# A third buffer for the filter's values, sines four steps behind their phases, and the second step's loads issued with the first step's

## The chip, the cores and the metric

The kernel runs on one core of a Trainium2 chip. The time is the device time of one execution in microseconds (us). The kernel before has a median of 3793.43 us over 7 executions (3792.16 to 3796.14). A profile records one execution: which instruction ran when on each engine, and what ended each wait. The engines are TensorE (PE: matrix products; PEld is its weight load), VectorE (DVE), ScalarE (ACT), GpSimd (POOL), and SyncE (SP), which does nothing here but start the DMA transfers. SP takes its instructions strictly in turn: a transfer whose wait is not over holds all that stand behind it (SPq in the profile's rows).

## The reference

```python
B, S, D = 4, 12480, 128
h_filt = (np.maximum(pos_emb @ w1, 0.0) @ w2) * np.exp(-0.01 * pos)[:, None]
u = x * v
Uf = np.fft.rfft(u, n=2 * S, axis=1)
Hf = np.fft.rfft(h_filt, n=2 * S, axis=0)
y = np.fft.irfft(Uf * Hf[None], n=2 * S, axis=1)[:, :S, :]
z = (x * y).reshape(B * S, D)        # 49920 rows of 128
h = z @ moe_w_in                     # 128 -> 2048
g = h * np.cos(h)
out = g @ moe_w_out                  # 2048 -> 128
```

A long convolution of `u` with a filter along the sequence, for each of 128 channels and 4 batches, and then a two-layer network with `h * cos(h)` between its layers.

## The kernel before

**The convolution by matrix products.** The Fourier transform over the sequence is done in two steps, each a set of matmuls with tables of sines and cosines: N1 = 96 by N2 = 120 points. Forward: the first step (`f1_units`, matmul at line 402) goes over 64 groups of two channels, called b here, and evicts each result from PSUM into the large tile `slots` (lines 415 to 422; for the filter into `ftile` and `slots`, lines 424 to 435). The second step (`f2_units`) goes over 48 pairs of frequencies k1: a matmul with a matrix `w` that also holds the twiddle factors (line 442), and the complex product with the filter's values `h` (lines 458 and 460 on DVE, the sum at 461 on POOL). Backward: `i1_units` (line 466) and `i2_units` (line 491) in the same manner; the latter's result is multiplied by `x` and written to the DRAM tensor `zd`.

**Stages in order.** 0 to about 62 us: layers that make the filter in time, in part beside `u = x * v` of batch 0 (lines 390 and 396). About 64 to 118 us: first step of the filter; the evictions go to ACT for a share of 0.53 of the b's and to DVE for the others. Beside it the last u tiles are made, and then the tables for the backward transform (`inverse_tables`): POOL makes the phases of ten sines (lines 200 to 217), and ACT does a sine of each (line 226). The class `Tables` keeps a list of phases that wait for their sine; when the list has `lag` entries, the oldest is put onto ACT's stream. One step of `inverse_tables` is taken for every fifth yield of the first step, so where a sine stands among ACT's evictions is set when the program is written out. About 122 to 168 us: first step of batch 0. About 168 to 274 us: `f2_both_units`, the second step of batch 0 and of the filter at once. There ACT and DVE make `w` (lines 289 and 291), PE multiplies both (lines 442, 445, 448), ACT evicts the filter's values to an SBUF tile `h` (line 614), DVE and POOL form the product, and SP writes `w` to `wd` (line 603) and `h` to `hd` (line 616) in DRAM, from where the later batches load them. `w` and `h` have two buffers each. About 274 to 340 us: `i1_units` of batch 0.

**The network and the other batches.** From about 340 us on, the network runs over 98 row tiles of 16 chunks each, one step per chunk: `moe_up` (matmul 725, ACT 728, DVE 731, POOL 734), one step later `moe_act` (ACT 739, DVE 741), and `LAG` = 4 steps later `moe_down` (matmul 750). With every step, the loop takes as many units of the convolution of the later batches as a running account (`owed`) allows; each unit says how many steps it is worth. So the order of every engine's stream is written out by hand, by generators, and no scheduler changes it. In that part the convolution uses three PSUM banks, `cv`. The entry into `f2_units` comes three times, near 756, 1579 and 2400 us.

**What f2_units does at its start.** `units` first runs `before(j)` for the first `ahead` = 2 indices, which issues loads of `w` and `h` on SP (lines 581 and 583), then yields, and in its loop issues those of index j + 2 while it does index j. Its pool has three buffers of each.

**How an output tile leaves.** `moe_evict` copies the accumulated tile to `ot`; `moe_store`, called at chunk 8 of the next row tile, transposes it (matmuls at line 126), copies it to `ob` on ACT (line 765) and issues the stores to `out` on SP (line 773). `ob` has one buffer. The load of the rows of `zd` for a later tile (line 709, `zb`) is issued at chunk 12.

Of the kernel before, what the change touches and what calls it, by code (L numbers as in the profile page):

```python
# [9 lines left out]
F32 = mybir.dt.float32  # L10
# [6 lines left out]
P = 128  # L17
# [13 lines left out]
def kernel(  # L31
# [46 lines left out]
    nc = tc.nc  # L78

    B, S, D = x.shape  # L80
    FO = pos_emb.shape[1]
    DFF = moe_w_in.shape[1]
    N1, N2 = 96, 120
# [15 lines left out]
    NFC = DFF // P  # L99
# [151 lines left out]

    def inverse_tables(pool):

        t = Tables(pool, nc.gpsimd, 2)
        part = t.whole([P, 1], [[1, 1]], channel_multiplier=1, name="part")
        part4 = t.whole([P, 1], [[1, 1]], base=1, channel_multiplier=4, name="part4")
        step = t.whole([P, P], [[1, P]], name="step")
        mid = t.whole([P, P], [[1, P]], base=-MID, name="mid")
        cs, rows, tw_t = back_tables(pool)
        yield from t.sines(step, part, N2, [(cs[:, 0, 0:H + 1], 1), (cs[:, 1, 0:H + 1], 0)],  # L260
                           eighths=slice(0, H + 1, H))
        yield from t.sines(step[:, 1:H], part, N2,
                           [(cs[:, 0, H + 1:], 0), (cs[:, 1, H + 1:], 1)])
        yield from t.sines(step, part4, 4 * N1,
                           [(rows[:, i, :], q) for i, q in enumerate((0, 1, 2, 3))])
        yield from t.sines(mid, part4, TURN, [(tw_t[:, 0, :], 1), (tw_t[:, 1, :], 0)],
                           eighths=slice(H - 1, N2, H))
        t.finish(1)
        for kept, made in ((csd, cs), (rowsd, rows), (twd, tw_t)):
            nc.sync.dma_start(kept[:, :, :], made[:, :, :])  # L270

    def back_tables(pool):

        cs = pool.tile([N2, 2, N2], F32, name="cs")
        rows = pool.tile([N1, 4, R], F32, name="rows")

        tw_t = pool.tile([N1, 2, N2], F32, name="tw_t")
        return cs, rows, tw_t
# [18 lines left out]
    def make_w(w, k1, **how):  # L297


        turn(w, even[:, 0, :], even[:, 1, :], tw_w[:, 0, k1:k1 + 1], tw_w[:, 1, k1:k1 + 1],  # L300
             **how)
# [98 lines left out]
    def f1_mm(ps, u, b, i):  # L400

        nc.tensor.matmul(ps[0:KE, i * 2 * N1:(i + 1) * 2 * N1], u[:, b, 0:KE, i],  # L402
                         c1[0:u.shape[0], :, :].rearrange("p r k -> p (r k)"),
                         start=True, stop=True)
# [161 lines left out]
    def f1_units(bank, u, share=0.5, evict=f1_evict):  # L566
        def mm(j, ps, i):
            if i == 0:
                ps = bank()
            f1_mm(ps, u, j, i)  # L570
            return ps

        return units(CB, F1_STEPS, lambda j: None, mm, lambda j, ps: evict(ps, j, share), 2)

    def f2_units(bank):
        with tc.tile_pool(name="there", bufs=3) as pool:
            ws, hs = {}, {}

            def before(j):
                ws[j] = pool.tile([KE, 2, N2], F32, name="w")  # L580
                nc.sync.dma_start(ws[j][:, :, :], wd[j, :, :, :])
                hs[j] = pool.tile([N2, 2, 2, D], F32, name="h")
                nc.sync.dma_start(hs[j][:, :, :, :], hd[j, :, :, :, :])

            def mm(j, ps, i):
                if i == 0:
                    ps = bank()
                f2_mm(ps, ws[j], 2 * j, i)
                return ps

            yield from units(N1 // 2, F2_STEPS, before, mm,
                             lambda j, ps: f2_product(pool, ps, hs.pop(j), 2 * j), 4)

    def f2_both_units(bank):

        with tc.tile_pool(name="both", bufs=2) as pool:
            ws = {}

            def before(j):
                ws[j] = pool.tile([KE, 2, N2], F32, name="w")  # L600
                for i in range(2):
                    make_w(ws[j][:, i, :], 2 * j + i, half=bank)
                nc.sync.dma_start(wd[j, :, :, :], ws[j][:, :, :])

            def mm(j, ps, i):
                if i == 0:
                    ps = bank(), bank()
                for filt in range(2):
                    f2_mm(ps[filt], ws[j], 2 * j, i, filt=filt == 1)
                return ps  # L610

            def after(j, ps):
                h = pool.tile([N2, 2, 2, D], F32, name="h")
                nc.scalar.activation(h[:, :, :, :].rearrange("p g r d -> p (g r d)"),
                                     ps[1][0:N2, :], AF.Copy, scale=1.0 / M)
                nc.sync.dma_start(hd[j, :, :, :, :], h[:, :, :, :])
                yield from f2_product(pool, ps[0], h, 2 * j)

            yield from units(N1 // 2, F2_STEPS, before, mm, after, 4, ahead=1)
# [69 lines left out]

    def forward_units(bank, back):  # L690

        yield from f1_units(bank, slots[0:R, :, :, :])
        yield from f2_units(bank)
        next(back)
        yield from i1_units(bank)

# [3 lines left out]
    def first_row(n):  # L700
        return min(R + (n - 1) * P, NROWS) if n else 0
# [54 lines left out]
        nc.scalar.copy(out=ot[:, 0:m], in_=accs.pop(n)[:, 0:m])  # L756
        return ot

    def moe_store(pool, n, ot):
        m = rows_of(n)  # L760
        pt = ps_h.tile([P, BANK], F32, name="ph")
        for i in range(G):
            transpose(pt[0:m, i * D:(i + 1) * D], ot[:, i * m:(i + 1) * m], ident)
        ob = pool.tile([P, 2, UA * D], F32, name="ob", bufs=1)
        nc.scalar.copy(out=ob[0:m, :, :].rearrange("p h n -> p (h n)"), in_=pt[0:m, :])
        row = first_row(n)
        while row < first_row(n + 1):
            b, g, n1 = row // R // NG, row // R % NG, row % R
            count = min(R - n1, first_row(n + 1) - row)
            first, _, second, _ = n2s(g)  # L770
            start = out[b * S + n1 * N2 + first, :]
            at = row - first_row(n)
            nc.sync.dma_start(
                bass.AP(tensor=start.tensor, offset=start.offset,
                        ap=[[N2 * D, count], [(second - first) * D, 2], [1, UA * D]]),
                ob[at:at + count, :, :])
            row += count

    with tc.manual_schedule():
        with tc.tile_pool(name="psum", bufs=8, space=PSUM) as psum, \  # L780
                ExitStack() as first:
            def bank():
                return psum.tile([P, BANK], F32, name="ps")
# [5 lines left out]
            aT = above.rearrange("p b j i -> p b (j i)")  # L789


            keep = first.enter_context(tc.tile_pool(name="keep", bufs=1, side="right"))
            w2_sb = keep.tile([P, 2 * D], F32, name="w2_sb")
            nc.gpsimd.memset(w2_sb[:, :], 0.0)
            with tc.tile_pool(name="layers", bufs=1, side="right") as pool:
                w1_sb = pool.tile([P, P], F32, name="w1_sb")
# [42 lines left out]
            for _ in first_u:  # L839
                for _ in range(2):  # L840
                    next(f1)
            with tc.tile_pool(name="tables", bufs=1) as pool:
                sines = inverse_tables(pool)
                for i, _ in enumerate(f1):
                    if i % 5 == 0:
                        next(sines, None)
                for _ in sines:
                    pass
# [39 lines left out]
        mpool = ctx.enter_context(tc.tile_pool(name="moe", bufs=2))  # L888
# [20 lines left out]
            next(conv)  # L909
        moe_turn(mpool, 0)  # L910
        steps = [(n, c) for n in range(NALL) for c in range(NFC)]
        hidden, gates, ots = {}, {}, {}
        for i in range(len(steps) + LAG):
            if i < len(steps):
                n, c = steps[i]
                if n == 0 and c == NFC // 2:
                    load(1)
                if c == NFC - 4 and n + 2 < NALL:
                    load(n + 2)
                hidden[i] = moe_up(mpool, n, c)  # L920
            if 0 <= i - 1 < len(steps):
                gates[i - 1] = moe_act(mpool, *hidden.pop(i - 1))
            if i >= LAG:
                pn, pc = steps[i - LAG]
                moe_down(pn, pc, gates.pop(i - LAG))
                if pc == NFC - 1:
                    ots[pn] = moe_evict(mpool, pn)
            if i < len(steps):

                if c == (LAG - 1 if n else NFC - 2) and n + 1 < NALL:  # L930
                    moe_turn(mpool, n + 1)
                if c == NFC // 2 and n - 1 in ots:
                    moe_store(mpool, n - 1, ots.pop(n - 1))
            owed += 1.0
            while owed > 0.0:
                owed -= next(conv, owed)
        for n in sorted(ots):
            moe_store(mpool, n, ots[n])
# [1 line left out]
_INS = ['x', 'v', 'pos_emb', 'w1', 'w2', 'moe_w_in', 'moe_w_out']  # L940
_OUTS = [((49920, 128), 'float32')]
# [25 lines left out]
```

## Time and profile before

| | us |
|---|---|
| median of 7 executions | 3793.43 (3792.16 to 3796.14) |
| the profiled execution's own time | 3792.16 |
| its span, first to last instruction | 3790.3 |
| mean granted clock of TensorE | 0.993 of full |
| h's evictions (line 614), 48 | 28.7 busy, 598 ns each |
| writes to hd and wd, 48 each | 240.0 KB and 116.2 KB each |
| matmuls of line 442 in the later batches | 173.6 busy, 381 ns each |
| SP's waits for ob before the stores, 56 | 1308.2 in all |

A row of the profile names the line, the engine, the operation, the tile written and those read, and how many; in brackets stands how long the engine was idle before it and what released it. In a list of waits a row reads: engine, tile and line that waited, what it waited for, and then the total us, how many times and the longest. A `DMA hd<-h` as releaser means that the transfer's arrival ended the wait. The granted clock (PEclk) is the share of full speed that the chip allowed TensorE. A line such as L126 or L226 is that of a helper that several callers use. Most matmuls appear as two records. Idle time of an engine counts only where nothing else sets the end of that stretch.

### The profile page before, as it was taken

To read this page: it belongs to the slowest core of one execution; us is meant where nothing else is said; L and a number is where in the kernel's file an instruction comes from. 1 tells how busy PE (TensorE), PEld (TensorE's weight loads), DVE (VectorE), ACT (ScalarE), POOL (GpSimd) and SP (SyncE) were. 2 spreads that over 40 slices of the span, in tenths; PEclk is the share of its full clock that TensorE was granted. 3 is DMA by queue.
4 is the path that set the end of the run, shared out by engine and by line. 5 is a ranking of instruction groups with operands and counts; after the bars stand their busy time and mean duration, and the time that the engine had idled before them with its cause. 6 is when DMAs were issued, how large, how long until landed. Compare 5 with 4: busy or idle time off the path is not lost.

```text
span 3790.3 us, 47246 instructions
## 1 busy us (share of the span) xinstructions
PE 3703.5 (98%) x13546; PEld 2109.3 (56%) x13546; DVE 2771.2 (73%) x5658; ACT 2519.7 (66%) x4683; POOL 2592.0 (68%) x2342
## 2 busy tenths in 40 slices
PE   7898999999999999999999999999999999999999
PEld 6777555645466555555565556555566544444444
DVE  8887887678876887778766787788765566666666
ACT  5756776766665557766655567666664677777777
POOL 6666886478854665688845664788644577777776
PEclk9999999999999999999999999999999999999999
DMA  6253541022201550122203540222105300000000
GB/s 166 73 175 100 150 149 52 12 80 75 76 23 54 176 174 20 36 79 78 61 12 104 180 122 12 62 78 78 42 12 163 91 18 22 17 18 22 17 21 15
DMA packets 209499, 276.14 MB, mean 73 GB/s; under 512 B 17111, under 2 KB 146535, under 8 KB 209111
## 3 DMA queue, kind: packets, MB, share of 16 engines
q1 hardware_dynamic: 209239, 273.12, 24.4%
q8 instruction: 109, 1.79, 0.2%
q14 instruction: 151, 1.24, 0.1%
HBM read 193.64 MB, written 79.42 MB: 72 GB/s over the span
## 4 chain that ended last, share of the span: by engine, by line
PE 82%; POOL 7%; DVE 4%; ACT 3%; DMA 2%; issue 2%; SPq 0%; POOLq 0%; ACTq 0%; DVEq 0%
PE ph L725 31%; PE acc L750 26%; PE cv L750 5%; PE cv L491 5%; PE cv L466 4%; POOL f L734 4%; PE cv L402 3%; PE cv L442 3%; PE ph L126 2%; PE ps L402 2%; DMA hd<-h 1%; DVE k L731 1%; ACT cs L739 1%; POOL tm L295 1%; PE ps L466 1%
## 5 line engine op out<-in xcount | busy, mean ns | idle before, releaser
L734 POOL TENSOR_TENSOR f<-a,k 128x512 f32<-128x512 f32 (+1 forms) x1568 | 1988.7, 1268 | 1057.1 <-DVE k L731 1054.4
L725 PE MATMUL ph<-at,w_in_sb 128*128 128x512 f32 (+1 forms) x3136 | 1601.7, 592 | 5.2 <-DVE gt L741 4.6
L728 ACT ACTIVATE a<-ph,quarter 128x512 f32<-128x512 f32 (+1 forms) x1568 | 1073.3, 685 | 761.3 <-PE ph L725 752.0
L750 PE MATMUL acc<-gt,w_out_sb 128*128 128x512 f32 (+1 forms) x2688 | 1373.8, 593 | 10.1 <-ACT ot L756 9.8
L741 DVE TENSOR_TENSOR gt<-ph,cs 128x512 f32<-128x512 f32 (+1 forms) x1568 | 1077.2, 687 | 318.9 <-ACT cs L739 292.4
L731 DVE TENSOR_SCALAR k<-a 128x512 f32<-128x512 f32 (+1 forms) x1568 | 769.5, 491 | 628.4 <-ACT a L728 607.6
L739 ACT ACTIVATE cs<-f 128x512 f32<-128x512 f32 (+1 forms) x1568 | 980.3, 625 | 333.4 <-POOL f L734 330.8
L750 PEld LDWEIGHTS acc<-gt,w_out_sb 128*128 128x128 f32 x2688 | 505.9, 189 | 663.4 <-issue 619.8
L725 PEld LDWEIGHTS ph<-at,w_in_sb 128*128 128x128 f32 x3136 | 554.4, 190 | 338.5 <-issue 269.7
L461 POOL TENSOR_TENSOR slots<-slots,t 120x256 f32<-120x256 f32 x384 | 311.7, 818 | 62.7 <-DVE t L460 27.0
L491 PEld LDWEIGHTS cv<-slots,tm 96*104 96x104 f32 x1920 | 240.9, 170 | 107.3 <-issue 84.1
L491 PE MATMUL cv<-slots,tm 96*104 96x128 f32 x1920 | 254.4, 275 | 8.5 <-DVE tm L291 4.9
L750 PE MATMUL cv<-gt,w_out_sb 128*128 128x512 f32 (+1 forms) x448 | 224.5, 583 | 0.7 <-DVE gt L741 0.7
L466 PEld LDWEIGHTS cv<-cs,slots 120*96 120x96 f32 x1536 | 176.7, 167 | 67.6 <-issue 65.7
L466 PE MATMUL cv<-cs,slots 120*96 120x120 f32 x1536 | 183.1, 266 | 0.0
L442 PE MATMUL cv<-slots,w 124*120 124x256 f32 x576 | 173.6, 381 | 6.6 <-DMA w<-wd 6.6
L442 PEld LDWEIGHTS cv<-slots,w 124*120 124x120 f32 x576 | 103.8, 184 | 130.6 <-issue 117.7
L402 PEld LDWEIGHTS cv<-c,slots 104*124 104x124 f32 x768 | 132.5, 192 | 71.2 <-issue 58.3
L402 PE MATMUL cv<-c,slots 104*124 104x192 f32 x768 | 151.2, 326 | 4.8 <-DVE gt L741 3.5
L750 PEld LDWEIGHTS cv<-gt,w_out_sb 128*128 128x128 f32 x448 | 84.9, 190 | 104.5 <-issue 99.5
L390 DVE TENSOR_TENSOR xt<-xt,vt 104x256 f32<-104x256 f32 x177 | 137.2, 782 | 0.2 <-DMA vt<-in_v_dram 0.2
L476 DVE TENSOR_TENSOR slots<-cv,other 96x240 f32<-96x240 f32 x384 | 133.7, 394 | 4.2 <-ACT other L474 4.2
(129 smaller groups left out, 2581.8 us busy)
## 6 DMA issues: line engine op xcount, KB each, us to landing
h<-hd SPq DMA_DIRECT2D x144, 240.0 KB
tm<-td SPq DMA_DIRECT2D x96, 312.0 KB
xt<-in_x_dram SPq DMA_DIRECT2D x120, 208.0 KB
vt<-in_v_dram SPq DMA_DIRECT2D x120, 208.0 KB
xs<-in_x_dram SPq DMA_DIRECT2D x120, 208.0 KB
zd<-zs SPq DMA_DIRECT2D x119, 208.0 KB
zb<-zd SPq DMA_DIRECT2D x96, 256.0 KB
w<-wd SPq DMA_DIRECT2D x144, 116.2 KB
```

Source lines behind the costliest of these rows:

```text
L402: nc.tensor.matmul(ps[0:KE, i * 2 * N1:(i + 1) * 2 * N1], u[:, b, 0:KE, i], c1[0:u.shape[0], :, :].rearrange("p r k -> p (r k)"), start=Tr ...
L442: nc.tensor.matmul(pi, w[:, i, :], parts[0:KE, :, k], start=True, stop=True)
L461: nc.gpsimd.tensor_tensor(y[:, r], y[:, r], t[:, r], op=op)
L466: nc.tensor.matmul(ps[0:N1, (i * 2 + r) * N2:(i * 2 + r + 1) * N2], parts[0:N2, r, :, b, i], cs[:, r, :], start=True, stop=True)
L491: nc.tensor.matmul(ps[0:R, i * D:(i + 1) * D], t[:, i, r, :], slots[0:N1, :, place, :], start=(r == 0), stop=(r == 1))
L725: nc.tensor.matmul(ph[:, 0:m], w_in_sb[:, c * P:(c + 1) * P], ats[n][:, 0:m], start=True, stop=True)
L728: nc.scalar.activation(a[:, 0:m], ph[:, 0:m], AF.Identity, bias=quarter[:, 0:1], scale=INV_TWO_PI)
L731: nc.vector.tensor_scalar(out=k[:, 0:m], in0=a[:, 0:m], scalar1=ROUND, scalar2=ROUND, op0=ALU.add, op1=ALU.subtract)
L734: nc.gpsimd.tensor_tensor(f[:, 0:m], a[:, 0:m], k[:, 0:m], op=ALU.subtract)
L739: nc.scalar.activation(cs[:, 0:m], f[:, 0:m], AF.Sin, scale=TWO_PI)
L741: nc.vector.tensor_tensor(gt[:, 0:m], ph[:, 0:m], cs[:, 0:m], op=ALU.mult)
L750: nc.tensor.matmul(accs[n][:, 0:m], w_out_sb[:, c, :], gt[:, 0:m], start=(c == 0), stop=(c == NFC - 1))
```

## The change

Four edits. In `f2_both_units`, `h` has three buffers instead of two; `w` keeps two. In `inverse_tables`, the list of waiting phases holds four entries instead of two, so each sine stands two entries later in ACT's stream, and at the end all that are left are put there together. The tile `w2_sb`, which the filter's layers use, moves to a pool on the other side of SBUF and is given back ahead of the tables, whose `turned` tile has five buffers instead of three. In `forward_units`, the generator of the second step is started ahead of the first step, so the first two pairs of loads of `w` and `h` are issued on SP before the first step's matmuls. And `moe_store` is split: transposes and the copy to `ob` stay at chunk 8 (`moe_back`), and the stores on SP are issued at chunk 10. The order of instructions on PE, DVE and POOL is the same in both kernels; on ACT only the ten sines stand elsewhere, and on SP only these loads and stores.

```diff
     def inverse_tables(pool):
-        t = Tables(pool, nc.gpsimd, 2)
+        t = Tables(pool, nc.gpsimd, 4)
...
-        t.finish(1)
+        t.finish(len(t.waiting))
...
             def after(j, ps):
-                h = pool.tile([N2, 2, 2, D], F32, name="h")
+                h = pool.tile([N2, 2, 2, D], F32, name="h", bufs=3)
...
     def forward_units(bank, back):
+        f2 = f2_units(bank)
+        next(f2)
         yield from f1_units(bank, slots[0:R, :, :, :])
-        yield from f2_units(bank)
+        yield from f2
         next(back)
         yield from i1_units(bank)
...
-    def moe_store(pool, n, ot):
+    def moe_back(pool, n, ot):
         m = rows_of(n)
         pt = ps_h.tile([P, BANK], F32, name="ph")
         for i in range(G):
             transpose(pt[0:m, i * D:(i + 1) * D], ot[:, i * m:(i + 1) * m], ident)
         ob = pool.tile([P, 2, UA * D], F32, name="ob", bufs=1)
         nc.scalar.copy(out=ob[0:m, :, :].rearrange("p h n -> p (h n)"), in_=pt[0:m, :])
+        return ob
+
+    def moe_store(n, ob):
         row = first_row(n)
...
-            keep = first.enter_context(tc.tile_pool(name="keep", bufs=1, side="right"))
-            w2_sb = keep.tile([P, 2 * D], F32, name="w2_sb")
+            keep = tc.tile_pool(name="keep", bufs=1)
+            w2_sb = keep.__enter__().tile([P, 2 * D], F32, name="w2_sb")
...
             for _ in first_u:
                 for _ in range(2):
                     next(f1)
+            keep.__exit__(None, None, None)
             with tc.tile_pool(name="tables", bufs=1) as pool:
...
-        hidden, gates, ots = {}, {}, {}
+        hidden, gates, ots, obs = {}, {}, {}, {}
...
                 if c == NFC // 2 and n - 1 in ots:
-                    moe_store(mpool, n - 1, ots.pop(n - 1))
+                    obs[n - 1] = moe_back(mpool, n - 1, ots.pop(n - 1))
+                if c == NFC // 2 + 2 and n - 1 in obs:
+                    moe_store(n - 1, obs.pop(n - 1))
...
         for n in sorted(ots):
-            moe_store(mpool, n, ots[n])
+            moe_store(n, moe_back(mpool, n, ots[n]))
```

## The prediction

> **What bounds the kernel now.** I read the page's busy rows and its slices first.
>
> ```profile
> PE 3703.5 (98%) x13546; PEld 2109.3 (56%) x13546; DVE 2771.2 (73%) x5658; ACT 2519.7 (66%) x4683; POOL 2592.0 (68%) x2342
> ...
> PE   7898999999999999999999999999999999999999
> ```
>
> TensorE (PE) is busy 98% of the 3790.3 us span: 3790.3 - 3703.5 = 86.8 us are idle, and the slices (94.8 us each) put most of that in the first 300 us and one dent near 760. In the last 3,000 us PE is the bound, so there only a gap of PE is worth anything; what the change can win lies in the early stages and in such gaps. So I looked at the three places that it touches: the stage that makes the filter's values (166 to 285 us), the tables stage (97 to 122 us), and the entry into the second step of later batches (about 756, 1579, 2400 us).
>
> **Part A, three buffers for h (line 613).** The stage's waits, from 166 to 285 us (total, times, longest):
>
> ```profile
> ACT h L614 <- DMA hd<-h: 17.3, 17, 1.4
> ...
> DVE slots L458 <- ACT h L614: 6.9, 19, 0.6
> ```
>
> ACT may not write h(j) before the write of h(j-2) to DRAM has landed; DVE's product then waits for h. The chain of waits from 190 to 212 us (start, length, what) shows it closing:
>
> ```profile
> 195.49 0.60 ACT h L614
> 196.12 3.28 DMA hd<-h
> 199.50 0.60 ACT h L614
> 200.42 3.89 DMA hd<-h
> 204.42 0.60 ACT h L614
> ```
>
> One turn of two steps is 0.60 plus a landing. From the semaphore events of the trace I took all 48 landings of hd: 2.4 to 4.06 us after the issue, median 3.18. A pair of steps at the median takes 0.60 + 3.18 = 3.8 us, less than the 4.0 us that DVE needs (below), so only the slow landings show. ACT's 17.3 us is not on the path by itself; DVE's is, because DVE paces the stage. Its row in the timeline: w at 199.48 and 201.51, and at 206.38, 208.40, 210.43, so 2.02 us a step where nothing stalls; h at 172.28 to 271.78 gives 99.5 us / 47 = 2.117 us on average. Excess: 47 x (2.117 - 2.02) = 4.5 us. A second count: DVE's gaps just before line 458 that end with h, thirteen of 0.15 us or more (.45 at 202.53 and .60 at 205.05 are two), add to 4.4 us; all 19 are 6.9, of which some start a step that is not late afterwards. With three buffers h(j) waits for h(j-3): three steps are 6.06 us against 0.60 + 4.06, so no landing seen is late. What is late next is w, which keeps two buffers: w(j+1) may be written when wd(j-1) has landed (2.73 to 4.03 us, median 2.88), and at 2.02 us a step it comes about 3.46 us after that issue. Four writes (200.09, 202.12, 238.04 and 240.06, at 3.58 to 3.76 us) would then be late by 0.1 to 0.3 us each, about 0.8 together at most 1.1, less where they fall in one run. So A is worth 4.5 less about half a us: **-4.0**, between -5 (all of both counts) and -2 (the writes, closer together, land later, and w takes over half).
>
> **Part B, the second step's first loads before the first step (lines 690-695).** PE's timeline at the first entry, and SP's there:
>
> ```profile
> 755.38 0.60 PE L126 MATMUL ph<-ident,ot 128*128 128x128 f32 x4
> 762.56 1.18 PE L442 MATMUL cv<-slots,w 124*120 124x256 f32 x2 [6.59 <-DMA w<-wd]
> 763.54 1.91 PE L725 MATMUL ph<-at,w_in_sb 128*128 128x512 f32 x2
> ```
> ```profile
> 756.85 1.16 SPq L773 DMA_DIRECT2D out_dram<-ob  x3
> 758.13 0.26 SPq L581 DMA_DIRECT2D w<-wd  x1
> 758.43 0.41 SPq L583 DMA_DIRECT2D h<-hd  x1
> ```
>
> The three stores wait for the copy into ob (ACT, after PE's transposes at 755.38); the loads of w stand behind them on SP, and PE reaches the step's first matmul before w lands. The whole run's waits hold exactly one wait of line 442 for w, of 6.6 us: the other two entries have none. In the changed order of instructions the first two pairs of loads stand ahead of the first step's matmuls for 64 b's, some 140 us earlier, and the third ahead of the store. So the 6.59 us go. With them goes a slow restart: the granted clock was 1.00 over 740 to 756 and 0.69 over 762 to 768, where two matmuls of L442 took 1.18 us (0.60 at 768.03) and two of L725 1.91 (1.02 before). Laying the same work out from 755.98 at the rows' full pace ends at 759.86, where the trace has 768.03: 8.2 us. Small waits of line 750 for its operand, hidden by the gap before, take back some tenths: **-7.9**, from -8.2 to -6.5 (stall alone). No engine but PE bounds this stretch, and its next work is 3,000 us without a gap, so the gain reaches the end whole.
>
> What the moved loads are queued before: on SP at about 607 us they wait until the second step's buffers are free of what used that memory, the last sums of u (line 396, about 616 us). Behind them stand an output store (634.34) and a load of zb (635.16): at most 9 us of waiting, with 18 us of room. Cost nothing; if the wait passed 20 to 30 us, PE would starve for zb.
>
> **Part C, sines four behind (lines 254, 268).** ACT stands still for 6.88 us before the first sine, since this is put ahead of its evictions:
>
> ```profile
> 100.84 0.26 ACT L226 ACTIVATE cs<-turned 120x61 f32<-120x61 f32 x1 [6.88 <-POOL turned L217]
> ...
> 118.35 0.30 ACT L226 ACTIVATE tw_t<-turned 96x120 f32<-96x120 f32 x1 [0.99 <-POOL turned L217]
> 120.55 0.30 ACT L226 ACTIVATE tw_t<-turned 96x120 f32<-96x120 f32 x1 [1.90 <-POOL turned L217]
> ```
>
> Four steps of lag take most of this away, but not the end. POOL starts the phases at 97.67, after the last u tile, and runs without a gap to 120.51: its ten phases set the last sine at 120.55 in both kernels. Two evictions of the filter stand behind that sine, and PE's next matmuls wait for the first of these:
>
> ```profile
> 122.07 5.15 PE L402 MATMUL ps<-c,slots 104*124 104x192 f32 x30 [2.96 <-ACT slots L410]
> ```
>
> So PE does its filter matmuls earlier and waits longer for the same point. Gain at the end: 0. By the rows (1.17 us for an ACT eviction, 1.37 for DVE's, 0.65 for the four matmul records of a b) PE would be done at about 114.8 and idle 7.3 us instead of 2.96. [...] The row: after 2.96 us of idleness the clock was 1.00 (119 to 127 us), so a mere repetition costs 0. [...] A cold b is 1.3 us (100 to 105 us, granted 0.51: eight records in 2.68 us, 0.335 each), a warm one 0.65 (111 to 114 us: 17 records in 2.75), and ACT behind it has only 0.27 us of slack, at 125.63; then ACT runs without a gap to 167.97 and starts the next stage. [...] The new gap resembles the 6.59 row, so I take +1.7; the range is -0.3 to +2.5. The moved pool (line 797) adds to POOL's first iota only a wait for PE work done long before: 0.
>
> **Part D, out store two steps later (moe_back, moe_store).** PE's transposes and ACT's copy stay where they are; only SP's stores move. SP waits 1308.2 us in all for ob, mostly after 2750 us with nothing behind. Before that a few loads (403.33, 482.51, 523.17 us, and PE's 0.60 at 2067.85 behind a store at 2060.97) stand behind such a store and come up to 1 us sooner. ob keeps one buffer, and the next copy into it is 14 steps after the store (14 x 1.7 us, two matmuls of L725 and two of L750 a step), while a store lands in a few us. **-0.3**, from -1.5 to +1.
>
> **Sum.** -4.0 - 7.9 + 1.7 - 0.3 = -10.5 us on the profiled execution: its span 3790.3 becomes 3779.8; with its 1.9 us around the span (3792.16 - 3790.3) 3781.7. That execution is the fastest of the seven; on the median, 3793.43 - 10.5 = 3782.9. I give **3782.5**.
>
> **Rivals.**
> - *A's wait is only handed on* (writes of w and h, closer together, share the same queues; waits of line 291 for wd take the place of line 614's). A gives -2 or less, and the restart of C costs its 2.5: -2 - 6.5 to -7.9 + 2.5 - 0.3, about 3787. For it: wd's landings reach 4.03 us and w has only 3.46 - 2.88 = 0.6 us of room over the median. Against it: only four of the later writes passed 3.46 us. Chance 0.2, most of it inside 0.2%.
> - *The sines gain* (they don't do what part C reckons): if POOL's phases ran faster once ACT and DVE go on, or the two evictions stood before the last sine in effect, up to 3 us of the 2.96 gap and of the cold start would go: 3782.9 - 1.7 - 3 = 3778. Against it: POOL has no gap in its timeline there. Chance 0.1.
> - *The change does nothing for B*: w lands late again, because the loads are still held on SP: -4.0 + 1.7 - 0.3 gives 3791. Against it: 140 us of lead. Chance 0.04.
> - *Slower*: the moved loads hold SP's queue. Place: the three entries near 607, 1440 and 2260 us. If the memory under their buffers comes free late, zb and the input loads behind wait, and PE's rows of L725 with them. It decides once the wait passes about 20 us plus what the rest gains, i.e. where three entries lose 6 us each, 18 in all: 3782.5 + 18 = 3800.5. What speaks for it: SP does its issues strictly in turn, and waits up to 43.9 us at others' heads. Against: the last user is done at 616. Chance 0.06.
>
> **How the numbers follow.** The forecast itself has 0.6. 0.2% of the time is 7.6 us, about what a measurement of this kernel can tell from no change: faster means below 3785.8. The forecast's own range is 3779 to 3786, from A's and C's bounds. Faster: 0.57 of it, the sines' 0.1 and 0.08 of the handed-on wait: 0.75. Same: 0.03 + 0.12 + 0.04 = 0.19. Slower 0.06. The range for 8 in 10 leaves out the slower case and the tail: 3776.5 to 3789.
>
> **What would show it.** A: between 166 and 285 us the waits of line 614 for hd gone, the step near 2.03 us, perhaps new waits of ACT (289) or DVE (291) for wd. B: no wait of line 442 for w, and the clock of 756 to 768 at 1.00. C: no 6.88 us before the first sine, the last sine as late after POOL's start as now, one longer gap of PE before batch 0's matmuls and a clock below 1.00 after it. D: the stores behind, nothing else. The prediction is wrong if the stage from 166 us keeps its 2.12 us a step, if PE's gap near 760 only moves, or if PE waits for zb near 616 to 640.

## The result, and the profile after

The changed kernel takes 3784.86 us (median of 14 runs, 3782.96 to 3788.72), the kernel before beside it 3795.54 us (34 runs, 3791.13 to 3799.3): a ratio of 0.9973, with a 95% interval of 0.9966 to 0.998, so about 10 us faster (7.6 to 12.9). A second group of runs gave 0.9975 (0.9966 to 0.9985). The profiled execution took 3785.13 us, its span is 3783.3, and its mean granted clock 0.993.

Four places changed. Both kernels have the same 13,546 weight loads on PE in the same order, so the n-th of one can be set beside the n-th of the other, and the difference of their starts tells where the time went. This table is worked out from the two traces (the index is that of the weight load, counted from 0):

| weight load | before, us | after - before, us | what lies between it and the row above |
|---|---|---|---|
| 446, first after PE's gap, batch 0's first step | 122.07 | -0.41 | |
| 500, the 54th after it | 130.79 | +2.29 | the restart: 2.71 lost |
| 709, start of the second step | 172.47 | +2.75 | 0.46 lost |
| 1142, near its end | 263.87 | -0.23 | the third buffer: 2.98 won |
| 3178, last ahead of the first entry | 754.95 | -0.46 | |
| 3188, after the entry | 765.89 | -8.80 | the wait for w: 8.34 won |
| 5000 | 1263.9 | -8.96 | |
| 5602 | 1408.3 | -6.43 | 2.5 lost |
| 13540 | 3784.3 | -7.00 | |

**The second step of batch 0.** The list of waits of the changed kernel from 166 to 285 us (engine, tile and line, what it waited for; total us, times, longest):

```profile
ACT h L614 <- DMA hd<-h: 32.2, 41, 1.4
...
DVE w L291 <- DMA wd<-w: 1.5, 2, 0.8
```

ACT waits for the write to hd more than before, 32.2 us instead of 17.3, and yet the stage is faster: DVE's wait for h, 6.9 us before, has no row any more. With three buffers ACT is ahead of DVE, and here a wait of the engine that is ahead costs nothing. DVE's gaps in the timeline show what is late next (idle time and releaser in brackets):

```profile
206.00 0.59 DVE L291 SCALAR_TENSOR_TENSOR w<-even,tw_w,ps 124x120 f32<-124x120 f32 x2 [0.66 <-DMA wd<-w]
...
243.07 0.59 DVE L291 SCALAR_TENSOR_TENSOR w<-even,tw_w,ps 124x120 f32<-124x120 f32 x2 [0.83 <-DMA wd<-w]
...
270.20 0.42 DVE L460 TENSOR_TENSOR t<-ps,h 120x256 f32<-120x256 f32 x1 [0.58 <-POOL slots L461]
...
272.21 0.42 DVE L460 TENSOR_TENSOR t<-ps,h 120x256 f32<-120x256 f32 x1 [0.59 <-POOL slots L461]
```

Twice the write of w is late, by 0.66 and 0.83 us. The writes of w land later than before: by the semaphore events (the marks that a finished transfer leaves in the trace), a median of 3.30 us after their issue instead of 2.88. In the last two steps, where no more w is made, DVE would go faster than its 2.02 us a step, and waits for POOL, which must be done with the single buffer of t.

**The first entry into the second step of a later batch.** PE's timeline, and SP's:

```profile
754.92 0.60 PE L126 MATMUL ph<-ident,ot 128*128 128x128 f32 x4
755.36 0.60 PE L442 MATMUL cv<-slots,w 124*120 124x256 f32 x2
```
```profile
615.89 0.26 SPq L581 DMA_DIRECT2D w<-wd  x1
616.20 0.35 SPq L583 DMA_DIRECT2D h<-hd  x1
616.59 0.30 SPq L581 DMA_DIRECT2D w<-wd  x1
616.94 0.35 SPq L583 DMA_DIRECT2D h<-hd  x1
633.89 0.73 SPq L778 DMA_DIRECT2D out_dram<-ob  x2
```

The matmul of line 442 follows the transposes at once. The loads went at 615.89, and the store behind them at 633.89, as before (634.34): the queue is not held.

**The sines.** ACT's first and last sine, PE's gap after them, and the busy time of the engines from 121 to 127 us (PE, PEld, DVE, ACT, POOL; granted clock; DMA share and GB/s):

```profile
100.44 0.26 ACT L226 ACTIVATE cs<-turned 120x61 f32<-120x61 f32 x1 [2.14 <-POOL turned L217]
...
120.14 0.30 ACT L226 ACTIVATE tw_t<-turned 96x120 f32<-96x120 f32 x1 [1.90 <-POOL turned L217]
```
```profile
121.66 8.67 PE L402 MATMUL ps<-c,slots 104*124 104x192 f32 x35 [7.09 <-ACT slots L410]
```
```profile
121.00:127.00 6.00, 5.34 (x17) 5.34 (x18) 1.18 (x3) 3.76 (x14) 0.00 (x0) 0.50 0.46 146
```

ACT's first stall is 2.14 instead of 6.88 us, the last sine is as late as before, and PE's gap is longer (7.09 us instead of 2.96), with half the clock after it (0.50 over 121 to 127 us).

**A new wait, near 1287 us**, in the stage where batch 1's last step (matmul 491) runs beside the making of batch 2's u. SP's timeline of the changed kernel, then PE's:

```profile
1279.23 0.84 SPq L778 DMA_DIRECT2D out_dram<-ob  x2
1280.12 0.41 SPq L711 DMA_DIRECT2D zb<-zd  x1
...
1281.37 0.33 SPq L660 DMA_DIRECT2D tm<-td  x1
```
```profile
1287.59 1.11 PE L491 MATMUL cv<-slots,tm 96*104 96x128 f32 x8 [1.45 <-DMA tm<-td]
```

and SP's of the kernel before around the same load of tm, the twentieth of each trace:

```profile
1280.84 0.84 SPq L773 DMA_DIRECT2D out_dram<-ob  x2
...
1283.39 0.34 SPq L660 DMA_DIRECT2D tm<-td  x1
...
1288.16 0.39 SPq L709 DMA_DIRECT2D zb<-zd  x1
...
1290.31 0.35 SPq L660 DMA_DIRECT2D tm<-td  x1
```

PE is 9.0 us earlier here, so the load at 1290.31 answers to the one at 1281.37. Before, the store went 9.5 us ahead of it, with another load of tm between, and zb's load 2.2 us ahead. Now store, zb (256 KB) and tm (312 KB) go within 2.2 us. By the semaphore events tm lands 6.1 us after its issue instead of 3.5, and PE waits for it.

### The profile page after: what moved, and what is told of

It is laid out like the page before. It is cut to its first block, busy times and chain, and to the rows that moved or that the text cites. A ratio compares the mean times of both kernels' runs of the same rounds, so it can differ in the third digit from the quotient of the medians.

```text
span 3783.3 us, 47244 instructions
## 1 busy us (share of the span) xinstructions
PE 3703.1 (98%) x13546; PEld 2109.7 (56%) x13546; DVE 2772.8 (73%) x5658; ACT 2524.7 (67%) x4683; POOL 2592.4 (69%) x2342
## 4 chain that ended last, share of the span: by engine, by line
PE 83%; POOL 7%; DVE 4%; ACT 2%; issue 2%; DMA 1%; SPq 0%; POOLq 0%; DVEq 0%; ACTq 0%
PE ph L727 31%; PE acc L752 27%; PE cv L752 5%; PE cv L491 5%; PE cv L466 4%; POOL f L736 4%; PE cv L402 3%; PE cv L442 3%; PE ph L126 2%; PE ps L442 1%; PE ps L402 1%; DVE k L733 1%; ACT cs L741 1%; POOL tm L295 1%; POOL slots L461 1%
```

## The experiments

Twelve runs were made. Those named "u" undo a part in the changed kernel, those named "o" do one part alone in the kernel before, those named "x" add something to the changed kernel, and "again" is the changed kernel itself. All ratios are to the kernel before on the same chip. The intervals of these twelve are 6 to 10 us wide, about as wide as the whole effect, so most verdicts on parts rest on stretches of the traces. Unless the text says otherwise, these lie between the same two weight loads of each trace, one execution of each kernel.

| run | median, us | ratio (95% interval) |
|---|---|---|
| u_sines | 3784.85 | 0.9965 (0.9951 to 0.9978) |
| u_h2 | 3790.22 | 0.9981 (0.9972 to 0.9989) |
| u_loads | 3786.49 | 0.997 (0.9959 to 0.9982) |
| u_store | 3785.38 | 0.9964 (0.9951 to 0.9976) |
| u_both | 3790.82 | 0.9991 (0.9982 to 1.0) |
| o_store | 3787.83 | 0.9974 (0.9964 to 0.9984) |
| o_loads | 3789.41 | 0.9976 (0.9967 to 0.9984) |
| o_sines | 3795.46 | 1.0001 (0.9992 to 1.001) |
| x_warm | 3784.54 | 0.9967 (0.9954 to 0.9979) |
| x_defer | 3779.5 | 0.9953 (0.994 to 0.9967) |
| x_defer2 | 3783.97 | 0.9968 (0.9955 to 0.998) |
| again | 3785.92 | 0.9975 (0.9966 to 0.9985) |

### Two buffers for h again (u_h2)

```diff
-                h = pool.tile([N2, 2, 2, D], F32, name="h", bufs=3)
+                h = pool.tile([N2, 2, 2, D], F32, name="h")
```

> The changed kernel with two buffers for h again. Theory: DVE's waits for h come back (5 to 7 us in the list of waits) and the stage from 166 us takes 2.09 us a step again instead of 2.02: 3.3 us slower than the changed kernel, about 3788. Rival (the wait was only handed on to the writes of w and h): 1.5 us slower or less, 3786.

DVE's waits are back (list of waits from 170 to 290 us):

```profile
ACT h L614 <- DMA hd<-h: 21.1, 21, 1.4
...
DVE slots L458 <- ACT h L614: 7.5, 20, 0.7
```

From DVE's first product to the end of its last, this stage takes 101.2 us here, and 100.7 to 101.4 in the kernel before and the three that do one other part alone. It takes 97.6 to 97.9 in six executions with three buffers (the changed kernel twice, u_sines, u_loads, u_store, u_both). The means are 100.98 and 97.74: the third buffer is worth **3.2 us**. By DVE's 47 step starts alone it is 99.6 to 95.7, 3.9 us; the other 0.7 is POOL's wait at the end.

The three kernels named "x" keep three buffers too. x_defer and x_defer2 take 97.6 and 97.5, but x_warm takes 99.15. Its list of waits from 166 to 285 us shows why:

```profile
DVE w L291 <- DMA wd<-w: 6.3, 9, 3.5
```

The longest of these nine, 3.5 us, lies ahead of the first product; the others lie in the stage. So in eight of nine executions the theory stands and the rival of 1.5 us or less falls, and in one nearly half of the gain was handed on to the writes of w. Why they were late so often there is open.

### The loads, the stores, and both (u_loads, u_store, u_both, o_loads, o_store)

```diff
# u_loads: the loads where they were
-        f2 = f2_units(bank)
-        next(f2)
         yield from f1_units(bank, slots[0:R, :, :, :])
-        yield from f2
+        yield from f2_units(bank)
# u_store: the stores where they were
-                if c == NFC // 2 + 2 and n - 1 in obs:
+                if c == NFC // 2 and n - 1 in obs:
# u_both: both.  o_loads, o_store: the kernel before with the moved loads, or the moved stores, alone
```

> The changed kernel with the second step's loads where they were (after the first step). Theory of the prediction: PE waits for w near 756 us again, 6 to 8 us slower, about 3793. Rival, from the order of SP's instructions: with the stores two steps later the loads stand ahead of the store even without being moved, so the store's move alone removes the wait: within 1 us of the changed kernel, 3785, no wait of line 442 for w.

> The changed kernel with the stores back at chunk 8, right after the copy. Theory: the early loads alone also remove the wait near 756 us, so nothing comes back there; and the store no longer falls next to zb's and tm's loads (PE's wait of 1.45 us for tm at 1287 us goes), so 0 to 2 us faster than the changed kernel: about 3784. Rival (the prediction's, stores out of the way of loads are a gain of 0.3): 3785.2. Rival (the store's move is what removed the wait): 3793.

Undone one at a time, neither part brought the wait back: 0.997 and 0.9964, and no wait of line 442 for w in either trace. So they were done alone, and undone together. (o_store also has w2_sb in its new pool.)

> The kernel before with the store's move alone (and w2_sb in its new pool). Theory (the moved store alone lets the loads of w pass): PE's wait of 6.6 us at 762 us is gone, 6 to 8.5 us faster than before, ratio 0.998. Rival (it needs the moved loads): the ratio is 1.000 within 0.0005, and the wait is there.

> The kernel before with the moved loads alone. Theory: the wait of 6.6 us and the slow restart go: 7.5 to 8.5 us faster than before, ratio 0.998; and since the stores are where they were, no new wait for tm: as fast as the stores' move alone or up to 1.5 us faster. Rival: the loads hold SP's queue near 607 us and a part of the gain is lost: 4 to 6 us faster.

> The changed kernel with the loads and the stores both where they were. Theory (either of the two moves removes the wait for w near 756 us, so that each undone alone showed nothing): PE's wait of 6.6 us at the first entry is back, the clock after it is below 1.00, and the kernel is 7.5 to 8.5 us slower than the changed kernel. Rival (the wait went for another reason, such as the shifted start): within 1 us of the changed kernel.

Each alone takes 9 to 10 us off the kernel before, and with both undone the wait is back. The median of u_both is 4.9 us above that of the changed kernel beside it (again), where 7.5 to 8.5 was expected; the two intervals overlap, so the size is taken from the traces. PE's timeline of u_both, then SP's:

```profile
754.41 0.60 PE L126 MATMUL ph<-ident,ot 128*128 128x128 f32 x4
761.90 1.18 PE L442 MATMUL cv<-slots,w 124*120 124x256 f32 x2 [6.89 <-DMA w<-wd]
```
```profile
755.88 1.17 SPq L776 DMA_DIRECT2D out_dram<-ob  x3
757.15 0.26 SPq L581 DMA_DIRECT2D w<-wd  x1
```

and SP's of o_store, where the loads were not moved in the program:

```profile
720.50 0.29 SPq L581 DMA_DIRECT2D w<-wd  x1
...
758.91 1.19 SPq L776 DMA_DIRECT2D out_dram<-ob  x3
```

The loads there need nothing that is late; they only stood behind a store that waited for ob. With the store issued two steps later they come first in SP's stream and go at 720.50, 37 us ahead of PE's first matmul of line 442 (757.88). From weight load 3178 to 3190 the trace has 11.80 us before, 11.70 in o_sines and 13.15 in u_both (the three with the wait), and 3.45 in all eleven others: **8.35 us** against the kernel before (8.25 and 9.70 against the other two), for either part, once.

**The stores' price.** The stretch from weight load 4200 to 5700 (about 1090 to 1440 us, where the new wait was seen) sorts the traces by the stores' place, whatever else they change:

| stores at | us from load 4200 to 5700 | mean |
|---|---|---|
| chunk 8: before, o_sines, o_loads, u_both, u_store | 345.18, 345.43, 345.42, 345.58, 346.28 | 345.6 |
| chunk 10: after, again, u_sines, u_h2, u_loads, o_store, x_defer, x_defer2, x_warm | 347.20, 348.38, 348.00, 348.34, 347.21, 348.70, 348.35, 348.09, 349.06 | 348.1 |

The groups do not overlap: the stores' move costs **2.6 us** there. PE's waits for tm from 1090 to 1440 us sort in the same way: 0.2 to 0.9 us in all with the stores at chunk 8, 1.8 to 3.8 us with chunk 10 (2.1 us apart in the mean). So tm's late loads are most of the cost; the rest of the 2.6 us is not traced. Earlier and later stretches show no such sorting; the last, from load 8700 to 13540, takes about 1531.3 or 1533.0 us without regard to the edits (see the end). So, by the traces, the loads' move alone would have been the better way to the same 8.35 us. The medians (u_store against the changed kernel, o_loads against o_store) are too close to tell.

### The sines (u_sines, o_sines, x_warm)

```diff
# u_sines: the changed kernel; o_sines: the kernel before, the other way round
-        t = Tables(pool, nc.gpsimd, 4)
+        t = Tables(pool, nc.gpsimd, 2)
# x_warm: the changed kernel, with 20 passes over the first half of batch 0's first b
-    def f1_units(bank, u, share=0.5, evict=f1_evict):
+    def f1_units(bank, u, share=0.5, evict=f1_evict, repeat=1):
...
-            f1_mm(ps, u, j, i)
+            for _ in range(repeat if j == 0 and i == 0 else 1):
+                f1_mm(ps, u, j, i)
...
-            beside(f1_units(bank, slots[0:R, :, :, :], 0.55),
+            beside(f1_units(bank, slots[0:R, :, :, :], 0.55, repeat=20),
```

> The changed kernel with the sines two behind again (all else changed). Theory: the later sines only lengthened PE's gap ahead of batch 0's first step (2.96 to 7.09 us) and the slow restart cost about 2.6 us there and some tenths in the next stage, so this kernel is 2.5 to 3.2 us faster than the changed one: about 3782, with PE's gap back at 3.0 us and the clock of 123 to 127 us at 1.00. Rival (the sines gain): slower than the changed kernel by 1 to 4 us. Rival (no matter): within 1 us of it.

> The kernel before with the sines four behind alone. Theory: PE's gap ahead of batch 0's first step grows from 2.96 to about 7.1 us with the same end, and the clock after it is 0.50; but the gap of 2.96 us lost the clock too in three of the executions seen (0.59, 0.72, 0.77), so the price is only 0 to 2.6 us in one execution and about 1 us on the median: ratio 1.0003, not to be told from 1. Rival (the prediction's +1.7 and more): 1.0005 to 1.0007. Rival (the sines gain): 0.999.

> The changed kernel, with the first half of batch 0's first b computed twenty times over instead of once (the same result into the same bank), so that PE is at work for about 6.2 us of its 7.1 us gap ahead of 121.7 us. It adds work and takes none away. Theory (the cold clock is the cost of the sines' move): the granted clock of 121 to 127 us is 1.00 instead of 0.50, batch 0's first step takes 42.0 us instead of 44.7, and the kernel is 2.5 to 3 us faster than the changed one: about 3782. Rival (the loss comes from how the evictions are queued, not from the clock): no gain, or 0.5 us slower for the repeated work, 3785 to 3786.

The expectation of u_sines failed in one point that matters. The gap went back to 2.93 us, but the clock did not come back (timeline of PE, then 121 to 127 us):

```profile
120.14 10.10 PE L402 MATMUL ps<-c,slots 104*124 104x192 f32 x43 [2.93 <-ACT slots L410]
```
```profile
121.00:127.00 6.00, 6.00 (x24) 6.00 (x23) 2.48 (x7) 2.74 (x9) 0.00 (x0) 0.59 0.45 131
```

From the first weight load after the gap to the 54th after it (446 to 500), by the length of the gap:

| gap | kernels | us | mean |
|---|---|---|---|
| 2.93 to 2.96 | before, o_store, o_loads, u_sines | 8.72, 10.41, 10.40, 11.57 | 10.28 |
| 6.5 to 7.1 | after, again, u_h2, u_loads, u_store, u_both, o_sines | 11.43, 11.27, 11.37, 12.01, 11.05, 10.82, 11.68 | 11.38 |

After the short gap the clock over 121 to 127 us was 1.00, 0.72, 0.77 and 0.59 in these four; after the long one 0.50 in all seven (u_h2, which comes 4 us later, over 125 to 131 us), save 0.55 in u_both. So the execution of the kernel before that was profiled first was the lucky one of four, and the longer gap costs **1.1 us** in the mean of these executions, not the 2.7 of the first comparison. With four and seven executions this is rough: the two groups overlap (11.57 in the first, 10.82 in the second). The ratio of o_sines, 1.0001, fits 1.1 us but cannot tell it from nothing.

The records of the granted clock in the 14 traces show where the clock was lost. They hold two values, full (1.0) and half (0.5). Within a trace every half-clock stretch starts on one grid of 3.41 us and lasts one or more of its steps (3.41 us in 61 cases, 6.83 in 29, longer in 24; the stretch at the kernel's end is left out): in the kernel before, the stretches that start at 62.52, 100.07, 168.33 and 274.15 us are 11, 20 and 31 times 3.413 us apart. Between 300 and 3775 us, the traces have 14,162 grid steps at full clock. In the 48 that a half-clock step follows PE was idle, by its matmul records, for 1.69 us or more, in the others for 1.65 us or less: in these traces the border lies between the two, near half a step (1.71 us). (Before 300 us the border is less sharp: from 95 us on it was lost from 1.23 us and kept up to 1.91.) In the kernel before the gap of 2.96 us fell across two steps, 1.43 us in one and 1.52 in the next, and the clock stayed; in o_store, o_loads and u_sines one step got 2.62, 1.98 and 1.93 us of idle time, and the clock was lost. By these figures a gap of 2.96 us keeps the clock only where it is split near its middle, at about one place in nine (an estimate: 2 x 1.67 - 2.96 = 0.38 of 3.41 us). A gap of 6.5 to 7.1 us is about two steps long and puts more than 1.69 us of idle time into at least one step, wherever it falls; in all seven executions with such a gap the clock was lost (0.50 to 0.55).

In x_warm PE is at work until 0.92 us ahead of the same point:

```profile
120.53 9.70 PE L402 MATMUL ps<-c,slots 104*124 104x192 f32 x58 [0.92 <-ACT slots L410]
```
```profile
121.00:127.00 6.00, 6.00 (x39) 6.00 (x38) 4.61 (x13) 5.40 (x18) 1.87 (x2) 1.00 0.46 131
```

The clock is 1.00. Against the kernel before, this kernel loses 0.24 us between the filter's matmuls at 89 us and 131 us (weight load 500 of the others), where the changed one loses 2.86. So the half clock is the cause, and the queue of evictions is not. Its ratio is too near the changed kernel's to be told from it.

### The sines moved out of the way (x_defer, x_defer2)

Phases are written into the tables, stored to DRAM as phases, loaded ahead of batch 0's second step, and turned into sines there (the edit, shortened):

```diff
+    def late_sines(cs, rows, tw_t):
+        for dst, n in ((cs[:, 0, 0:H + 1], N2), (cs[:, 1, 0:H + 1], N2), (cs[:, 0, H + 1:], N2),
...
+            nc.scalar.activation(dst, dst, AF.Sin, scale=TWO_PI / n)
+            yield
...
-        t.finish(len(t.waiting))
...
-            for _ in f2_both_units(bank):
-                pass
+            sines = late_sines(cs, rows, tw_t)
+            for i, _ in enumerate(f2_both_units(bank)):
+                if i % 8 == 5:
+                    next(sines, None)
...
# conversion of the network's first weights beside batch 0's first step:
-                        if i % 14 == 0:
+                        if i % every == 0 and i >= start:   # x_defer: 12, 24; x_defer2: 8, 40
```

> The changed kernel with the ten sines taken out of the filter's stage: POOL writes the phases into the tables themselves, these go to DRAM as phases, come back ahead of the second step, and ACT does the sines in place there, one in every eighth unit of that stage, where it has idle time; the conversion of the network's first weights begins 24 units later in batch 0's first step. Theory (the last sine, held by POOL's phases, is what the filter's last evictions and batch 0's first step wait for): batch 0's matmuls begin at about 114.5 instead of 121.7 us without a slow restart, so 7 to 10 us faster than the changed kernel: 3775 to 3778. Rival (POOL's phases hold the next stage anyway, through the conversion or the memory of the tables): within 2 us of the changed kernel.

> The kernel with the sines done in the second step's stage, as in the run x_defer, but the conversion of the network's first weights spread otherwise: from unit 40 on, every eighth (there: from 24 on, every twelfth). Theory (that kernel reached the start of batch 0's first step 10 us early and lost half of it to the conversion's tail, a wait of 3.4 us of DVE for the last write of these weights and a gap of 7.4 us of PE): the second step begins some 4 us sooner, and the kernel is 8 to 11 us faster than the changed kernel, ratio 0.994 to the one before. Rival (DVE's work in that stage, evictions and conversion, sets its end whatever the spread): as x_defer, 0.9953.

PE's timeline of x_defer, and DVE's:

```profile
111.12 15.94 PE L410 MATMUL ps<-c,slots 104*124 104x192 f32 x96
...
166.09 1.18 PE L450 MATMUL ps<-slots,w 124*120 124x256 f32 x2 [7.37 <-DVE w L299]
```
```profile
165.64 1.09 DVE L299 SCALAR_TENSOR_TENSOR w<-even,tw_w,ps 124x120 f32<-124x120 f32 x4 [3.44 <-DMA wind<-power]
```

Batch 0's first step starts at 111.12 instead of 121.66, with no gap and the clock at 1.00: the last sine, held by POOL's phases, was what PE waited for. At weight load 500 this kernel is 10.4 us ahead of the kernel before. Three quarters of it go again. In the rest of the first step, where DVE now has the conversion beside its evictions, 5.1 us are lost (weight load 695); another 2.7 go at the second step's first matmul (166.09, and 168.76 before), which waits for the conversion's last write. At weight load 3178 it is 3.6 us ahead of the kernel before and so 3.2 ahead of the changed one, where 7 to 10 was expected. Its ratio, 0.9953 (18 us less than the kernel before beside it), is the lowest of all, but its interval touches that of the changed kernel, and so much is not in its trace, that of the slowest of its five executions.

x_defer2 was to win that loss back and did the opposite. The rival of its expectation is nearer, that DVE's work sets the end of that stage, though it forecast no loss. With the conversion at every eighth unit, DVE has evictions and conversion in one stretch and PE stops at each of them (PE's timeline):

```profile
145.78 3.18 PE L410 MATMUL ps<-c,slots 104*124 104x192 f32 x16 [1.33 <-DVE slots L420]
149.96 3.18 PE L410 MATMUL ps<-c,slots 104*124 104x192 f32 x16 [1.00 <-DVE slots L420]
```

4.18 us for 16 records that take 3.18; at the end of the first step it is 1.95 us behind the kernel before, having been 9.5 ahead. A spread between the two, and x_defer with the stores back at chunk 8, were not tried.

### The changed kernel again

> The changed kernel itself, as a measure beside the three others of this group: ratio 0.9973 to the kernel before, as measured, within its own interval.

It held (0.9975), with the same marks in the trace: gap 7.09 us, clock 0.50, no wait for w.

## Why the prediction was right, and where its steps were not

The time is right: -10.5 us forecast, -10.7 measured. The four terms are less so:

| part | forecast, us | measured, us | by |
|---|---|---|---|
| A, third buffer | -4.0 (-5 to -2) | -3.2 | u_h2, two groups of traces |
| B, early loads | -7.9 (-8.2 to -6.5) | -8.35, with D, once | o_loads, o_store, u_both |
| C, sines later | +1.7 (-0.3 to +2.5) | +1.1 in the mean | eleven traces, x_warm |
| D, stores later | -0.3 (-1.5 to +1) | the same -8.35 alone, and +2.6 later | o_store, five traces against nine |
| sum | -10.5 | -7.9 (with B and D's -8.35 once) | |

The sum of the traced parts, -7.9, lies inside the interval of the whole (7.6 to 12.9 us faster), but 2.8 us short of its middle. What makes up the rest is open: the stretch from load 8700 on varies by 1.7 us between executions by itself, and the first profile of the kernel before was one of its fastest executions (the two first profiles are 7.0 us apart). That the total came out to 0.2 us is luck, then; that it came out in the range is not.

**A.** The mechanism held: h's wait for its write was on DVE's path, and w's write is late next. By DVE's step starts the size held too, 3.9 us for 4.0. The term left out is the end of the stage: there DVE had been waiting for h, and without this it waits for POOL, 0.58 and 0.59 us in the rows above, so the stage as a whole gains 3.2. The writes of w took more than the sum's half us: DVE's waits for them add to 0.7 to 1.5 us in the six executions, because they landed later (a median of 3.30 us instead of 2.88, above), as the lower end of the range had it. One sign that the prediction named was wrong: the waits of line 614 for hd were to be gone, since no landing was slower than three steps of DVE. They grew from 17.3 to 32.2 us: ACT, with a buffer more, runs ahead of DVE until the write of h three steps back holds it. The row that tells is DVE's wait for h, which is gone.

**B and D.** The step that failed is "only SP's stores move", with its -0.3 in part D. With the store two steps later in SP's stream, what had stood behind it went first, and among this were the loads of w, at 758.13 us in the kernel before and at 720.50 in o_store, whose 6.6 us were the largest single wait of the change. The prediction counted them under B alone. Its sum was not hurt, because the two parts remove one wait and not two; a reader who had costed both by what each removes would have had -16. In the other direction, D's range ended at +1 and the price was 2.6: it asked what stood behind the store in its old place, and not what stands next to it in the new one, zb's load two chunks later and tm's load right behind. Of the signs it named for D, "the stores behind, nothing else" failed with this.

**C.** That the end of the stage does not move, since POOL's phases set it, held to 0.4 us, and so did the longer gap (7.09 us for 7.3). Against the row ("after 2.96 us the clock was 1.00") the prediction took it that the new gap loses the clock, rightly (0.50 after 7.09 us). The size that it put into the sum, +1.7, was the author's estimate, and no run shows it: the first two traces were 2.71 us apart over the restart, and the runs showed 1.1 us in the mean (11.38 us after the long gap, 10.28 after the short one). The row itself was a single execution, and three others with the same gap lost the clock (0.72, 0.77 and 0.59). In these traces the loss went with the idle time in one step of the grid of 3.41 us (1.69 us or more, above), and so with where the short gap fell. So the price of the change was the difference of two chances, about 1.1 us, and not the whole restart.

**The rivals.** The wait handed on to w: in kind yes, at 0.7 to 1.5 us, and in x_warm at nearly half of the gain. The sines gain: no. The queue held at 616 us: no; the store behind the moved loads went when it had gone before.

## What to carry to other kernels

In a queue that runs in order, as SP's did here, ask for every moved transfer what it overtakes and what overtakes it, and what it lands beside; two edits that free the same waiting instruction are worth one of them, which only both undone can show. A row that says "this gap cost nothing" is one draw where the clock depends on when the gap falls (1.00, 0.72, 0.77 and 0.59 after the same gap here): read it in more than one execution before it goes into a sum, and ask how a gap lies to the grid of the clock's records (3.41 us in these traces). And when an engine waits for another, look for what holds the last of the things waited for: here POOL's phases, ahead of two evictions on ACT, cost ten us at the start of the next step, which a longer lag within the same stretch did not touch. Most of these ten were lost again to the next wait, so a start that is earlier is worth only what the stage behind it can use.

## What the runs showed that was not expected

- The clock after the same gap of 2.93 to 2.96 us of PE was 1.00, 0.72, 0.77 and 0.59 over 121 to 127 us in four executions; after 6.5 to 7.1 us it was 0.50 in six of seven and 0.55 in the other.
- A store of one tile, zb's 256 KB and tm's 312 KB issued within 2.2 us: tm landed 6.1 us after its issue, and PE waited 1.45 us for it. With the store 9.5 us ahead of the same load it landed after 3.5 us, in time.
- The end of the kernel, from weight load 8700 to 13540, takes one of two lengths, 1.7 us apart, without regard to the edits. The traces show where: near 2690 to 2700 us PE is idle for 0.45 us and then for 1.46 us in all 14. In six (again, o_loads, o_store, u_h2, x_defer, x_warm) the granted clock over the 4 us after the second gap is 0.57 to 0.59, and these have the longer end; in the other eight it is 1.00. In the six both gaps put 1.80 to 2.01 us of idle time into one step of the grid, in the eight at most 1.65.
